# Attention and spectral mixing: the second group's weights as pairs of modes in rows of 12 KB

## The chip, the cores and the metric

The kernel runs on one core of one Trainium2 chip. The metric is device time in microseconds (us), the median of several runs; profiles come from one profiled execution, whose own time is given beside its span. Engines: PE (matmuls; PEld are its weight loads), DVE, ACT and Pool (elementwise work), SP (here it only issues DMAs). The 16 DMA engines move data between HBM and the on-chip memory of 128 partitions.

## What is computed

Sliding-window attention with a linear bias, then a mixing of its output in the frequency domain. q, k, v are [8, 8, 576, 64] (batch, head, position, depth), w_r and w_i are [64, 512, 512] (mode, in, out), w_ch is [512, 512], all float32.

```
attn[b,h] = softmax(q k^T / 8 - slope_h * |i - j|, only 0 <= i - j < 128) v
x = attn with heads side by side              # [8, 576, 512]
X = rfft(x, axis=1)                           # modes 0..63 are used
Yr = Xr w_r - Xi w_i ;  Yi = Xr w_i + Xi w_r  # per mode a 512 x 512 matrix
y = irfft(Y) ;  u = x + y
out = u + max(u w_ch, 0)
```

## The kernel before, in words

**Two groups of rows.** Heads come in four pairs, and a pair of heads is 128 of the 512 columns of x. Group 0 is the first pair, group 1 the other three (`GROUPS`, line 19). The mixing of group 0 needs only x's first 128 columns, so its weights (rows 0 to 127 of each mode's matrix) are loaded and used while the attention of group 1 still runs; the weights of group 1 (rows 128 to 511, 100.7 MB) come afterwards. All weights together are 134 MB, q, k and v 28 MB.

**Stages.** (a) `_slot` (line 537) is one step of the attention: scores (L431), exponentials on ACT (L437), masks on DVE (L445), transposes (L372, evacuated on ACT, L382), products with v (L462) and normalising on DVE (L480). Pool casts q, k and v to bf16 (`_cast`, L362). A slot also takes one step of the waiting spectra (`_spectrum1`) and at most one tile of group 0's modes (`_modes`, called with `w0` or `w1`). (b) After the last slots, the loop of lines 190 to 203 takes group 1's modes one after another, and between them fills PE with x times w_ch (`_xt`, four transposes L658, and `_xw`, L678 and L680, split by ACT and DVE into `hl`, L684 and L685), with the steps of the inverse transform's matrix (`_ft_steps`) and with the parts of the result that early modes allow (`_z_early`, L700 and L703). (c) `_finish` makes the output tiles and stores them.

**Spectra.** `_spectrum1` multiplies a batch's x by the cosine and sine matrix F on PE (L521), for group 1 in three steps a = 0, 1, 2 per batch, since the partition p of the result holds row 128 + 3p + a. After the third, DVE copies the spectrum (L528, real and imaginary) and its negated imaginary part (L529) to `Xlast` in bf16. Those of the last two batches come at the end of the attention, all in one slot.

**Modes.** `_modes` multiplies a mode's weights with the spectra: 4 blocks of outputs times A rows per partition (A = 3 in group 1) times w_r and w_i, so 24 matmuls with 128x128 weights and 16 columns (2 parts by 8 batches), added up in PSUM (`acc`). At the ends of blocks of modes the sums go to `ZTa` (float32, ACT, L645) in group 0, and with those added to `ZT` (bf16, DVE, L651) in group 1.

**The order of the work.** Every engine does its instructions in the order in which they are written (`manual_schedule`, line 95), SP's DMAs among them. The weights have a ring of three buffers for w_r and three for w_i (`RING`, 6 KB per partition each). `_load_w` (line 582) issues one DMA for w_r and one for w_i of a tile, 768 KB each: three modes of group 0 (rows of 2 KB in HBM), or one mode of group 1 (6 KB in a row: three rows of the matrix for each partition). A load waits until PE has used what was in its buffer. w_ch comes in four loads of 256 KB in four of the last slots of the attention (`_load_wch`, L602), and Pool casts them in four slots further on (`_cast_wch`, L606), before stage (b).

**The end.** Between the last four modes stand filler matmuls (`_idle`, L612, ten, ten, ten and five) whose results are not used.

Of the kernel before, what the change touches and what calls it, by code (L numbers as in the profile page):

```python
# [16 lines left out]
P = 128  # L17
# [16 lines left out]
def kernel(  # L34
# [28 lines left out]
    for grp in GROUPS:  # L63
        mg = ROWS // len(grp)
        n = NM // mg
        sizes = [mg] * n
        if NM % mg:
            sizes.insert(12, NM % mg)
        tiles.append([(sum(sizes[:i]), z) for i, z in enumerate(sizes)])
    g.ends = [{sum(t) for t in tiles[0][1::2]}, set(range(MB, NM, MB)) | {NM - 4, NM - 2}]  # L70

# [6 lines left out]
    g.FT = persist.tile([P, 4, S], BF16)  # L78
# [3 lines left out]
    g.wch = persist.tile([P, 4, DM], BF16)  # L82
    g.W, g.two, g.acc = {}, {}, {}
    g.X = [None] * len(GROUPS)
    g.X[-1] = persist.tile([P, len(GROUPS[-1]), 3, B, NM], BF16, name="Xlast")
# [9 lines left out]
    with tc.manual_schedule(engines={ET.SP, ET.PE, ET.Activation, ET.DVE, ET.Pool}):  # L95
        with ExitStack() as wctx:
            g.wpool = wctx.enter_context(tc.tile_pool(name="wpool", bufs=RING))
# [3 lines left out]
            with ExitStack() as actx:  # L101
# [3 lines left out]
                g.mask = cp.tile([P, H, 512], BF16)  # L105
                g.vns = [cp.tile([P, 2 * ST, 2, 72], BF16, name=f"vn{i}") for i in range(2)]
# [8 lines left out]
                todo = list(tiles[0])  # L115
                spare = todo.pop(0)
                loaded = (g.first[1] + LA) // 2
                for d in range(loaded):
                    _load(g, d)
                    if loaded - 2 <= d:  # L120
                        _load_w(g, 0, *todo.pop(0))
# [17 lines left out]
                with tc.tile_pool(name="spare", bufs=1, side="right") as sp:  # L139
                    _load_w(g, 0, *spare, pool=sp)  # L140
                    _load_w(g, 0, *todo.pop(0))
                    for n in range(n1, start + 1):
# [3 lines left out]
                        _slot(g, n, [], [(0, *spare)] if n == start else [])  # L146
                zx = ctx.enter_context(tc.tile_pool(name="zx", bufs=1, side="right"))
                g.ZTa = zx.tile([P, 4, 2, NM, 8], FP32)

                line = [(j, *t) for j in range(len(GROUPS)) for t in tiles[j]]  # L150
                _modes(g, 0, *tiles[0][1])
                _load_w(g, *line[RING + 1])
                ahead = RING + 2
                counts = [0, 1, 0, 1, 0, 1, 0, 1, 1, 0, 1] + [1] * (N - start - 12) + [1, 1, 1, 1]
                work, todo = {}, list(tiles[0][2:])
                for n in range(start + 1, N + 2 + TAIL):
                    work[n] = [(0, *todo.pop(0)) for _ in range(counts[n - start - 1])]
                assert not todo
                for n in range(start + 1, N + 2 + TAIL):
# [4 lines left out]
                    for _ in w:  # L164
                        _load_w(g, *line[ahead])
                        ahead += 1
                    h = (len(w) + 1) // 2
                    _slot(g, n, w[:h], w[h:])
                    if N - 7 <= n < N - 3:
                        _load_wch(g, n - N + 7)  # L170
                    if N - 2 <= n < N + 2:
                        _cast_wch(g, n - N + 2)
            zp = ctx.enter_context(tc.tile_pool(name="zpool", bufs=1, side="right"))
            g.ZT = zp.tile([P, 4, 4, 2, 16, 8], BF16)
# [4 lines left out]
            for t in line[ahead:]:  # L179
                _load_w(g, *t)  # L180
            with ExitStack() as xctx:
# [5 lines left out]
                todo, done, k = list(tiles[last]), 0, 0  # L187
                ftq = _ft_steps(g, xt, xps)
                xT = _xt(g, 0, xt, xps)
                while done < NM - 4:  # L190
                    m0, mg = todo.pop(0)
                    _modes(g, last, m0, mg, last=True)
                    done = m0 + mg
# [19 lines left out]
            for m0, mg in todo:  # L213
                _modes(g, last, m0, mg, last=True)
                if NM - 4 <= m0 < NM - 1:
                    _idle(g, BUSY)
# [61 lines left out]
def _consts2(g):  # L278
    nc = g.nc
    nc.gpsimd.tensor_tensor(  # L280
        out=g.ident2, in0=g.ident_b[:, 0:64], in1=g.ident_b[:, 64:128], op=ALU.add)
    for vn in g.vns:
        nc.gpsimd.memset(vn[:, :, :, g.D : g.D + 1], 1.0)
# [12 lines left out]
def _ft_steps(g, pool, psum):  # L296
# [7 lines left out]
    def begin():  # L304
# [4 lines left out]
        box.FTn = pool.tile([P, S], BF16, tag="FTn", name="FTn", bufs=1)  # L309
# [180 lines left out]
def _spectrum(g, d):  # L490
# [3 lines left out]
    if s == GROUPS[j][-1]:  # L494
        g.spectra += [(j, c, a) for c in (b, b + 1) for a in range(len(GROUPS[j]))]


def _spectrum1(g, j, b, a):
# [7 lines left out]
    X = g.X[j]  # L506
    nb = 4 // A
# [16 lines left out]
    if a < A - 1 or not own and b < g.B - 2 and k < nb - 1:  # L524
        return
    b0 = b - k
    if k == 0:
        nc.vector.tensor_copy(X[:, :, 1:3, b0], xt[:, 0])  # L528
        nc.vector.tensor_scalar_mul(X[:, :, 0, b0], xt[:, 0, :, 1], -1.0)  # L529
        return  # L530
    for a in range(A):
        xi = xt[:, 0 : k + 1, a].rearrange("p b i m -> p i b m")
        nc.vector.tensor_copy(X[:, a, 1:3, b0 : b + 1], xi)
        nc.vector.tensor_scalar_mul(X[:, a, 0, b0 : b + 1], xi[:, 1], -1.0)


def _slot(g, n, w0, w1):
# [16 lines left out]
    for w in w0:  # L554
        _modes(g, *w)
# [20 lines left out]
    if old:  # L576
        _av(g, d - 1, e, av)
    for w in w1:
        _modes(g, *w)


def _load_w(g, j, m0, mg, pool=None):
    nc = g.nc
    A = len(GROUPS[j])
    rows = slice(GROUPS[j][0] * P, (GROUPS[j][0] + A) * P)
    t = []
    for tag, src in (("wr", g.w_r), ("wi", g.w_i)):
        w = (pool or g.wpool).tile([P, ROWS, g.DM], FP32, tag=tag, name=f"{tag}{j}_{m0}")
        w = w[:, 0 : mg * A].rearrange("p (m a) e -> p m a e", a=A)
        nc.sync.dma_start(  # L590
            out=w.rearrange("p m a e -> p m (a e)"),
            in_=src[m0 : m0 + mg, rows].rearrange("m (p a) e -> p m (a e)", a=A))
        t.append(w)
    for i in range(mg):
        g.W[j, m0 + i] = (t[0][:, i], t[1][:, i])


def _load_wch(g, i):

    t = g.qpool.tile([P, g.R, g.D], FP32, tag="qk"[i % 2], name=f"wchf{i}")  # L600
    g.wchf = getattr(g, "wchf", []) + [t.rearrange("p r d -> p (r d)")[:, 0 : g.DM]]
    g.nc.sync.dma_start(out=g.wchf[i], in_=g.w_ch[P * i : P * i + P])  # L602


def _cast_wch(g, i):
# [234 lines left out]
```

## Time and profile before

| | before |
|---|---|
| median of 3 runs (lowest to highest) | 445.91 us (444.88 to 446.86) |
| the profiled execution: its time, its span | 446.81 us, 445.0 us |
| busy, share of the span: PE / PEld / DVE / ACT / Pool | 74% / 49% / 49% / 47% / 23% |
| read from HBM, written | 163.58 MB, 9.44 MB |
| loads of weights, 768 KB each: w_r, w_i | 85, 85 (and one of 256 KB each) |
| from issue to landing, median: w_r, w_i | 8.3 us, 9.7 us |
| PE waits for weights: w_r, w_i (L634, matmuls) | 14.0 us, 53.5 us |
| PE busy, 176 to 360 us | 112.8 of 184 us |

The profile's lines name a line of the kernel, an engine, an operation and out<-in with their shapes; "x24" counts instructions. A wait is put down to what ended it. The clock is TensorE's granted clock as a share of full speed. Slices are fortieths of the span, 11.1 us each; a digit is the busy share in tenths. A group's mean is the duration of one instruction; matmuls overlap, so that one of 0.19 us can follow another after 0.03 us.

### The profile page before, as it was taken

How to read it: one execution, taken by the hardware profiler on the slowest of the kernel's cores; microseconds unless marked ns; L12 is line 12 of the kernel's file. 1: busy time of each engine (PE TensorE's matmuls, PEld its weight loads, DVE VectorE, ACT ScalarE, POOL GpSimd, SP SyncE). 2: the span in 40 equal slices, each digit the busy share in tenths (PEclk: the TensorE clock that was granted, in tenths of full speed). 3: DMA queues.
4: the chain of work that ended last, by engine and by line, in shares of the span. 5: the costliest groups of instructions: out<-in, count | busy, mean ns of one | idle time of the engine just before them, and what ended most of it. 6: DMA issues, size and time to landing. Idle time of an engine off the chain costs nothing.

```text
span 445.0 us, 11009 instructions
## 1 busy us (share of the span) xinstructions
PE 327.6 (74%) x4626; PEld 217.1 (49%) x4654; DVE 219.2 (49%) x396; ACT 207.1 (47%) x313; POOL 101.6 (23%) x151
## 2 busy tenths in 40 slices
PE   2778889889979977467764656656665488869995
PEld 1445666666757654334443333333333355535553
DVE  6467867788758733242232323333233334512885
ACT  4799968999979501121322212212122132311884
POOL 8644535555533102000000000000000000000883
PEclk9999988999989855685566556566556669969999
DMA  8999989999999999999999999999999999992688
GB/s 294 395 389 385 404 321 399 392 404 405 406 406 402 406 409 404 417 423 425 422 423 425 419 415 418 426 423 423 424 423 423 425 410 417 416 422 122 252 313 288
DMA packets 55217, 173.73 MB, mean 390 GB/s; under 512 B 4992, under 2 KB 4992, under 8 KB 55168
## 3 DMA queue, kind: packets, MB, share of 16 engines
q1 hardware_dynamic: 55168, 173.04, 97.7%
q8 instruction: 36, 0.59, 0.5%
q14 instruction: 13, 0.11, 0.1%
HBM read 163.58 MB, written 9.44 MB: 389 GB/s over the span
## 4 chain that ended last, share of the span: by engine, by line
DMA 50%; PE 26%; ACT 12%; DVE 8%; issue 3%; SPq 1%; POOL 0%; ACTq 0%; POOLq 0%
DMA wi<-in_moe_w_i_dram 50%; PE acc L634 7%; ACT att L437 5%; ACT T L382 4%; DVE att L445 3%; PE mm L667 2%; PE idle L612 2%; PE tqk L372 2%; PE sc L431 2%; PE y L667 2%; PE xw L680 2%; PE av L462 1%; PE av L401 1%; DVE x_sb L480 1%; PE tp L658 1%
## 5 line engine op out<-in xcount | busy, mean ns | idle before, releaser
L684 ACT CAST hl<-xw 64x512 bf16<-64x512 f32 x72 | 41.8, 580 | 163.6 <-PE xw L680 126.1
L634 PEld LDWEIGHTS <-wi 128*128 128x128 bf16 x1024 | 65.7, 105 | 73.6 <-DMA wi<-in_moe_w_i_dram 71.7
L685 DVE TENSOR_TENSOR hl<-xw,hl 64x512 bf16<-64x512 f32 x72 | 49.6, 689 | 85.5 <-ACT hl L684 85.4
L634 PE MATMUL acc<-Xlast,wi 128*128 128x16 bf16 x768 | 55.9, 194 | 48.6 <-DMA wi<-in_moe_w_i_dram 48.5
L634 PEld LDWEIGHTS <-wr 128*128 128x128 bf16 x1024 | 70.7, 106 | 37.2 <-DMA wr<-in_moe_w_r_dram 26.4
L806 POOL TENSOR_TENSOR o<-r,ys 128x512 f32<-128x512 f32 x18 | 22.5, 1279 | 243.7 <-DVE r L798 242.3
L634 PE MATMUL acc<-Xlast,wr 128*128 128x16 bf16 x768 | 63.2, 194 | 19.4 <-DMA wr<-in_moe_w_r_dram 13.5
L445 DVE TENSOR_TENSOR att<-att,mask 128x1024 bf16<-128x1024 bf16 x64 | 55.9, 873 | 36.9 <-ACT att L437 36.6
L437 ACT ACTIVATE att<-sc 128x1024 bf16<-128x1024 f32 x64 | 66.7, 1043 | 9.9 <-PE sc L431 8.7
L382 ACT COPY T<-tqk 128x640 bf16<-128x640 bf16 x92 | 65.6, 767 | 1.7 <-PE tqk L372 1.7
L680 PE MATMUL xw<-wch,xT 128*128 128x512 bf16 x122 | 54.7, 577 | 4.9 <-issue 3.1
L372 PE MATMUL tqk<-ident_b,b 128*128 128x128 bf16 x432 | 39.4, 233 | 10.6 <-POOL b L362 6.4
L660 DVE COPY xT<-tp 128x512 bf16<-128x512 bf16 x36 | 15.2, 423 | 51.8 <-PE tp L658 50.8
L372 PEld LDWEIGHTS <-b 128*128 128x128 bf16 x432 | 27.3, 104 | 22.2 <-issue 11.0
L362 POOL CAST b<-v 128x576 bf16<-128x576 f32 x32 | 27.0, 871 | 17.6 <-issue 8.5
L680 PEld LDWEIGHTS <-xT 128*128 128x128 bf16 x144 | 19.0, 138 | 23.5 <-issue 21.6
L431 PE MATMUL sc<-T,T 64*128 64x256 bf16 (+2 forms) x320 | 26.9, 266 | 1.7 <-ACT att L437 1.0
L362 POOL CAST b<-q 128x576 bf16<-128x576 f32 x32 | 21.5, 699 | 28.9 <-issue 28.9
L362 POOL CAST b<-k 128x576 bf16<-128x576 f32 x32 | 22.0, 714 | 16.3 <-issue 8.5
L462 PE MATMUL av<-vn,att 128*128 128x65 bf16 (+1 forms) x576 | 25.3, 204 | 0.4 <-DVE vn L405 0.2
L462 PEld LDWEIGHTS <-att 128*128 128x128 bf16 (+1 forms) x576 | 21.3, 106 | 3.5 <-issue 0.2
L480 DVE TENSOR_TENSOR x_sb<-av,rec 128x512 bf16<-128x512 f32 x32 | 22.1, 692 | 1.1
(102 smaller groups left out, 437.8 us busy)
## 6 DMA issues: line engine op xcount, KB each, us to landing
wr<-in_moe_w_r_dram SPq DMA_DIRECT2D x85, 768.0 KB, 8.3
wi<-in_moe_w_i_dram SPq DMA_DIRECT2D x85, 768.0 KB, 9.7
q<-in_q_dram SPq DMA_DIRECT2D x32, 288.0 KB, 7.5
k<-in_k_dram SPq DMA_DIRECT2D x32, 288.0 KB, 6.1
v<-in_v_dram SPq DMA_DIRECT2D x32, 288.0 KB, 7.0
out_dram<-o SPq DMA_DIRECT2D x32, 256.0 KB, 3.0
wchf<-in_moe_w_ch_dram SPq DMA_DIRECT2D x4, 256.0 KB, 10.7
out_dram<-o SPq DMA_DIRECT2D x8, 128.0 KB, 2.7
```

The source lines that it names most:

```text
L362: g.nc.gpsimd.tensor_copy(u.b[w][:, :, e], u.raw[w][e])
L372: g.nc.tensor.transpose(u.tp[:, r - r0], u.b[w][:, r].rearrange("p u d -> p (u d)"), g.ident_b)
L382: copy(u.T[w].rearrange("c h (p r) -> c (h p) r", r=g.R)[:, :, r0:r1], u.tp[:, 0 : r1 - r0].rearrange("c r p -> c p r"))
L431: nc.tensor.matmul(sc[:, e, c0 : c0 + nq], lhsT=kT[es, h, _start(kt) : _start(kt) + P], rhs=qT[es, h, kt * P : kt * P + nq], start=True, s ...
L437: nc.scalar.activation(a, sc, AF.Exp, scale=1.0 / math.sqrt(g.D))
L445: nc.vector.tensor_tensor(out=a, in0=a, in1=m, op=ALU.mult)
L462: nc.tensor.matmul(av[o, h, t * (D + 1) : (t + 1) * (D + 1)], lhsT=u.att[min(kt // 2, 1), h][:, f, c0 : c0 + m], rhs=vn[:, g.ST * h + kt, ...
L480: nc.vector.tensor_tensor(out=xo, in0=avv[:, :, 0:4, 0:D], in1=rec[:, :, 0:4].unsqueeze(-1).broadcast_to([P, 2, 4, D]), op=ALU.mult)
L634: nc.tensor.matmul(acc[:, et, :, m - c0, :], lhsT=(wr, wi)[k][:, a].bitcast(BF16)[:, 1::2][:, et * P : (et + 1) * P], rhs=X[:, a, 1 - k : ...
L680: nc.tensor.matmul(xw, lhsT=xT[:, dt], rhs=g.wch[:, dt], start=(dt == 0 and g.way[n] != "q"), stop=(dt == 3))
L684: nc.scalar.copy(g.hl[hi, n, h], xw[hi])
L685: nc.vector.tensor_tensor(out=g.hl[lo, n, h], in0=xw[hi], in1=g.hl[hi, n, h], op=ALU.subtract)
```

## The change

Group 1's weights are loaded as items of one matrix (w_r or w_i) and two modes, m and m + 1, 1.5 MB in one DMA: partition 2q takes rows 6q to 6q + 5 of mode m, and partition 2q + 1 the same rows of mode m + 1, each 12 KB in a row in HBM. A matmul with such weights sums over both modes' rows, so the spectra are laid out with zeros: for the columns of an even mode the odd partitions hold zero, and the other way round. `_expand` makes this from the old layout (`Xc`) with a 0/1 matrix (`pick`): two matmuls, a copy on DVE and a negation on Pool for each half of the six rows, so that a batch of group 1 takes five steps of spectra, not three, and a slot may take a second one. `_pair_modes` then does a pair in 48 matmuls with 32 columns, all of w_r first, then all of w_i.

The ring is now one tile of three slots of 12 KB, the same bytes. An item is a pair's w_r or w_i, or three modes' w_r and w_i of group 0, which are still two loads with rows of 2 KB. `_send` is written behind the matmuls that free a slot. The last item is loaded in two halves.

To make room, `FT` and `wch` move to memory that is free only after the attention, `ZT` lies inside `ZTa`, and w_ch is loaded in one DMA of 1 MB behind the first pair of group 1 (`_wch`), into a part of `hl` that is filled last; Pool casts it from there. The first `_xt` moves behind that too. The filler matmuls are divided anew (ten, ten, three, five), and there are eleven output buffers instead of twelve. The core of the diff (old bodies that stand above are left out):

```diff
+    tiles.append([])
     g.ends = [{sum(t) for t in tiles[0][1::2]}, set(range(MB, NM, MB)) | {NM - 4, NM - 2}]
+    tiles[1] = [(m, w) for m in range(0, NM, 2) for w in range(2)]
...
-    g.X[-1] = persist.tile([P, len(GROUPS[-1]), 3, B, NM], BF16, name="Xlast")
+    g.X[-1] = persist.tile([P, 2 * len(GROUPS[-1]), 3, B, NM], BF16, name="Xlast")
...
-            g.wpool = wctx.enter_context(tc.tile_pool(name="wpool", bufs=RING))
+            wpool = wctx.enter_context(tc.tile_pool(name="wpool", bufs=1))
+            g.wring = wpool.tile([P, RING, 2 * ROWS * DM], FP32)
+            g.line = [(j, *t) for j in range(len(GROUPS)) for t in tiles[j]]
+            g.sent, g.used = 1, 0
...
+                g.pick = cp.tile([P, 2, 2, P], BF16)
+                g.Xc = cp.tile([P, 2, 3, 2, NM], BF16)
...
-                    for _ in w:
-                        _load_w(g, *line[ahead])
-                        ahead += 1
                     h = (len(w) + 1) // 2
                     _slot(g, n, w[:h], w[h:])
-                    if N - 7 <= n < N - 3:
-                        _load_wch(g, n - N + 7)
-                    if N - 2 <= n < N + 2:
-                        _cast_wch(g, n - N + 2)
+                    _send(g)
+            g.ZT = g.ZTa.bitcast(BF16).rearrange("p e k a m (b t) -> p e k (a m) b t", t=2)[..., 0]
+            g.FT = zp.tile([P, 4, S], BF16)
+            g.wch = zp.tile([P, 4, DM], BF16)
...
-            for t in line[ahead:]:
-                _load_w(g, *t)
...
-                todo, done, k = list(tiles[last]), 0, 0
+                todo, done, k = list(range(0, NM, 2)), 0, 0
                 ftq = _ft_steps(g, xt, xps)
-                xT = _xt(g, 0, xt, xps)
+                xT = None
                 while done < NM - 4:
-                    m0, mg = todo.pop(0)
-                    _modes(g, last, m0, mg, last=True)
-                    done = m0 + mg
+                    m0 = todo.pop(0)
+                    _pair_modes(g, m0)
+                    _send(g)
+                    done = m0 + 2
+                    if m0 == 0:
+                        _wch(g)
+                        xT = _xt(g, 0, xt, xps)
...
-            for m0, mg in todo:
-                _modes(g, last, m0, mg, last=True)
-                if NM - 4 <= m0 < NM - 1:
-                    _idle(g, BUSY)
+            for m0 in todo:
+                _pair_modes(g, m0)
+                _send(g)
...
+    nc.gpsimd.memset(g.pick, 0.0)
+    one = g.ident_b.rearrange("p (q t) -> p q t", t=2)
+    for h in range(2):
+        for t in range(2):
+            nc.gpsimd.tensor_copy(
+                g.pick[:, h, t].rearrange("p (q t) -> p q t", t=2)[:, :, t], one[:, :, h])
...
-        box.FTn = pool.tile([P, S], BF16, tag="FTn", name="FTn", bufs=1)
+        box.FTn = g.hl[:, len(g.seq) - 5].rearrange("p h d -> p (h d)")[:, 0:S]
...
-        g.spectra += [(j, c, a) for c in (b, b + 1) for a in range(len(GROUPS[j]))]
+        g.spectra += [(j, c, a) for c in (b, b + 1) for a in range(len(GROUPS[j]) + 2 * j)]
...
+    if a >= A:
+        _expand(g, X, b, a - A)
+        return
...
+    if j:
+        nc.vector.tensor_copy(g.Xc[:, b % 2], xt[:, 0])
+        return
     b0 = b - k
-    if k == 0:
-        nc.vector.tensor_copy(X[:, :, 1:3, b0], xt[:, 0])
-        nc.vector.tensor_scalar_mul(X[:, :, 0, b0], xt[:, 0, :, 1], -1.0)
-        return
-    for a in range(A):
-        xi = xt[:, 0 : k + 1, a].rearrange("p b i m -> p i b m")
-        nc.vector.tensor_copy(X[:, a, 1:3, b0 : b + 1], xi)
-        nc.vector.tensor_scalar_mul(X[:, a, 0, b0 : b + 1], xi[:, 1], -1.0)
+    xi = xt[:, 0 : k + 1, 0].rearrange("p b i m -> p i b m")
+    nc.vector.tensor_copy(X[:, 0, 1:3, b0 : b + 1], xi)
+    nc.vector.tensor_scalar_mul(X[:, 0, 0, b0 : b + 1], xi[:, 1], -1.0)
+def _expand(g, X, b, h):
+    nc = g.nc
+    A = len(GROUPS[-1])
+    if b == g.B - 1 and h:
+        xz = g.ps2.tile([P, 2, 512], FP32, tag="sc", name="xzl")[:, 0]
+    else:
+        xz = g.ps2.tile([P, 512], FP32, tag="xt", name="xz")
+    xz = xz[:, 0 : 2 * A * g.NM].rearrange("p (a i m) -> p a i m", a=A, i=2)
+    for t in range(2):
+        nc.tensor.matmul(
+            xz.rearrange("p a i m -> p (a i) m")[:, :, t::2], lhsT=g.pick[:, h, t],
+            rhs=g.Xc[:, b % 2].rearrange("p a i m -> p (a i) m")[:, :, t::2],
+            start=True, stop=True)
+    X = X[:, A * h : A * h + A]
+    nc.vector.tensor_copy(X[:, :, 1:3, b], xz)
+    nc.gpsimd.tensor_scalar_mul(X[:, :, 0, b], X[:, :, 2, b], -1.0)
...
+    if g.spectra and g.spectra[0][0]:
+        _spectrum1(g, *g.spectra.pop(0))
...
+        _modes(g, 0, *w)
+def _load_w(g, i, t):
+    sync = g.nc.sync
+    j, m, n = g.line[i]
     A = len(GROUPS[j])
     rows = slice(GROUPS[j][0] * P, (GROUPS[j][0] + A) * P)
+    if j == 0:
+        t = t.rearrange("p (w m e) -> p w m e", w=2, e=g.DM)
+        for w, src in enumerate((g.w_r, g.w_i)):
+            sync.dma_start(
+                out=t[:, w, 0:n], in_=src[m : m + n, rows].rearrange("m p e -> p m e"))
+            for x in range(n):
+                g.W[j, m + x, w] = t[:, w, x : x + 1]
+        return
+    src = (g.w_r, g.w_i)[n][m : m + 2, rows].rearrange("m (q r) e -> q m r e", r=2 * A)
+    t = t.rearrange("p (r e) -> p r e", e=g.DM)
+    h = A if i == len(g.line) - 1 else 2 * A
+    for r in range(0, 2 * A, h):
+        sync.dma_start(
+            out=t[:, r : r + h].rearrange("p r e -> p (r e)"),
+            in_=src[:, :, r : r + h].rearrange("q m r e -> q m (r e)"))
+    g.W[j, m, n] = t
+def _send(g, n=RING):
+    while n and g.sent < min(len(g.line), max(g.used, 1) + RING):
+        _load_w(g, g.sent, g.wring[:, (g.sent - 1) % RING])
+        g.sent += 1
+        n -= 1
+def _wch(g):
+    nc = g.nc
+    raw = g.hl[:, len(g.seq) - 4 :].rearrange("p n h d -> p (n h d)").bitcast(FP32)
+    raw = raw.rearrange("p (c d) -> p c d", c=4)
+    nc.sync.dma_start(out=raw, in_=g.w_ch.rearrange("(c p) d -> p c d", c=4))
+    for i in range(4):
+        nc.gpsimd.tensor_copy(g.wch[:, i], raw[:, i])
...
+            for k in range(c0 // 16, m // 16 + 1):
+                a, z = max(c0, 16 * k), min(m + 1, 16 * k + 16)
+                nc.scalar.copy(
+                    g.ZTa[:, :, k, :, a % 16 : a % 16 + z - a].rearrange("p e a m b -> p e a (m b)"),
+                    acc[:, :, :, a - c0 : z - c0].rearrange("p e a m b -> p e a (m b)"))
...
+def _pair_modes(g, m):
+    nc = g.nc
+    j = len(GROUPS) - 1
+    X = g.X[j]
+    A = 2 * len(GROUPS[j])
+    ends = g.ends[j] | {g.NM}
+    if m == 0 or m in ends:
+        g.acc[j] = (m, g.mpsum.tile([P, 4, 2, 8, 8], FP32, tag="acc", name="acc"))
+    c0, acc = g.acc[j]
+    late, end = m >= g.NM - 4, m == g.NM - 2
+    steps = [(0, et, a) for et in range(4) for a in range(A)]
+    if end:
+        steps += [(1, et, a + h) for h in (0, A // 2) for et in range(4) for a in range(A // 2)]
+    else:
+        steps += [(1, et, a) for et in range(4) for a in range(A)]
+    n = len(steps)
+    for i, (k, et, a) in enumerate(steps):
+        if late and 2 * i == n:
+            _idle(g, BUSY // 3 if end else BUSY)
+        if end and 4 * i == 3 * n:
+            _idle(g, BUSY // 2)
+        nc.tensor.matmul(
+            acc[:, et, :, m - c0 : m - c0 + 2, :],
+            lhsT=g.W[j, m, k][:, a].bitcast(BF16)[:, 1::2][:, et * P : (et + 1) * P],
+            rhs=X[:, a, 1 - k : 3 - k, :, m : m + 2].rearrange("p c b m -> p c m b"),
+            start=(i == 0), stop=(i == n - 1))
+    g.used += 2
+    if m + 2 in ends:
+        k, ms = c0 // 16, slice(c0 % 16, m % 16 + 2)
+        dst = g.ZTa[:, :, k, :, ms].rearrange("p e a m b -> p e a (m b)")
+        o = g.ZT[:, :, k].rearrange("p e (a m) b -> p e a m b", a=2)[:, :, :, ms]
+        nc.vector.tensor_tensor(
+            out=o.rearrange("p e a m b -> p e a (m b)"),
+            in0=acc[:, :, :, 0 : m + 2 - c0].rearrange("p e a m b -> p e a (m b)"),
+            in1=dst, op=ALU.add)
+    if late and not end:
+        _idle(g, BUSY)
...
-                o[j] = pool.tile([P, g.DM], FP32, tag="o", bufs=12, name="o")
+                o[j] = pool.tile([P, g.DM], FP32, tag="o", bufs=11, name="o")
```

## The prediction

> **What bounds the kernel now.** I read first the slices of the span, then a table by stage, then the chain of work that ended last.
>
> ```profile
> DMA  8999989999999999999999999999999999992688
> GB/s 294 395 389 385 404 321 399 392 404 405 406 406 402 406 409 404 417 423 425 422 423 425 419 415 418 426 423 423 424 423 423 425 410 417 416 422 122 252 313 288
> DMA 50%; PE 26%; ACT 12%; DVE 8%; issue 3%; SPq 1%; POOL 0%; ACTq 0%; POOLq 0%
> ```
>
> The DMA engines are busy through 36 slices (up to 400 us), and half of the chain is transfers. The rate has two levels: about 405 GB/s, and about 422 once only the second group's weights move. The table by stage (columns: window, length, busy us of PE, PEld, DVE, ACT, POOL, clock, DMA share, GB/s) says the same:
>
> ```profile
> 60.00:68.00 8.00, 6.79 (x107) 5.37 (x103) 3.94 (x10) 4.53 (x7) 2.67 (x3) 0.66 0.82 290
> 128.00:163.00 35.00, 31.20 (x536) 23.43 (x534) 23.72 (x48) 21.84 (x30) 7.91 (x12) 0.79 1.05 405
> 176.00:360.00 184.00, 112.76 (x1422) 70.07 (x1440) 57.87 (x103) 36.84 (x66) 0.00 (x0) 0.61 1.02 422
> 403.00:408.00 5.00, 4.87 (x64) 2.92 (x62) 0.04 (x1) 0.00 (x0) 0.00 (x0) 1.00 0.17 68
> ```
>
> So up to 403 us the time is bytes over rate, plus the holes in which the queue runs dry (one is at 60 to 68). Work on an engine costs nothing while the queue is fed, and its full length where it lets the queue drain. From 408 on PE, ACT and DVE share the end, which the change leaves nearly alone.
>
> **Rows of 12 KB.** From 128 us rows of 2 KB move at 405 GB/s, from 176 us rows of 6 KB at 422. Per engine (one of 16) that is 16 x 2048 / 405 = 80.9 ns and 16 x 6144 / 422 = 232.9 ns a row. The extra 4096 B take 152.0 ns (0.0371 ns a byte, 431 GB/s in all), which leaves 4.9 ns per row. A row of 12288 B then takes 461 ns, so 426.5 GB/s. The second group has 64 modes x 2 x 384 x 512 x 4 B = 100.7 MB: 238.5 us now, 236.0 after: **-2.5 us**. Bounds: no gain if such a row is moved in pieces (0), and 436 GB/s, the best single microsecond that I found (400 to 401 us), -7.6. The Trainium skill, DMA: Bandwidth & Descriptors, section Where 436 GB/s comes from, puts the ceiling of the 16 ports at 435 GB/s; by it at most 7.1 us could be won, and the 422 measured here stands within 3% of it.
>
> **w_ch is loaded late.** Before, its four 256 KB pieces go out from 127 to 141 us and Pool has cast the last by 152, 20 us ahead of the first use. Now one 1 MB load is put on SP's queue behind pair 0's two sends, and PE's first two x·w_ch products (L680) stand between pair 0 and pair 2. PE, in order, waits for the casts; behind it wait pair 2's matmuls, and SP's next send waits for those. What is in the queue by then are three items of 1.5 MB (3.7 us each) and w_ch (2.6 us at 405): 13.8 us, then nothing. The DMA engines idle from w_ch's last byte until the next item's first byte:
>
> ```profile
> L606 POOL CAST wch<-wchf x4: 611/616/617, 138.0 to 151.4; 128x512 bf16<-128x512 f32 x4
> 171.15 0.59 PE L658 MATMUL tp<-ident_b,x_sb 128*128 128x128 bf16 x4
> 171.54 1.91 PE L680 MATMUL xw<-wch,xT 128*128 128x512 bf16 x4
> 173.24 0.22 PE L634 MATMUL acc<-Xlast,wr 128*128 128x16 bf16 x1
> wchf<-in_moe_w_ch_dram SPq DMA_DIRECT2D x4, 256.0 KB, 10.7
> out_dram<-o SPq DMA_DIRECT2D x8, 128.0 KB, 2.7
> ```
>
> The last two lines (KB each, us from issue to landing) show that a load behind a full queue waits its turn: 256 KB took 10.7 us there, and 128 KB took 2.7 on the emptier queue of the end. The steps: landing after the last byte 0.7 (2.7 less 0.3 for the bytes and 1.7 for the start; the start is from the run's first load, issued at 0.73, whose window 0 to 4 us moved 0.67 MB, 1.7 us' worth, so bytes came from 2.3 on; I take 1.7); four casts of 0.615, 2.5; the first product's last matmul, 0.4; next transposes 0.4 (171.15 to 171.54); second product 1.7 (171.54 to 173.24, at the 0.5 clock granted there); 24 matmuls on pair 2's w_r, 0.75 (as from 170.42 to 171.15); SP 0.1; start 1.7. Sum **+8.3**. Bounds 5.5 (no start-up or landing time beyond the issue) and 10.5 (one more product's worth). The old cover, 20 us, is all gone.
>
> **Expanding the spectra.** Per batch two steps: two matmuls (192 columns), a DVE copy of 128x384 (0.55, row L528), a Pool negation; DVE's own negation (0.35, L529) goes, its first copy stays but goes to Xc. In the attention these 16 steps lie beside saturated transfers: SP waits there mostly for the DMA itself, ACT is the full engine, and loads land 8 to 11 us after issue, so a lag of some us is covered. Not covered is the last one. Now batches 6 and 7 take 163.55 to 168.09 on PE, and then group 0's last item frees its slot (SP issues at 168.99). After: spectrum 2.25, copy 0.65, expand 0.45, copy 0.6 (the PSUM tile is shared), expand 0.45, spectrum 2.3, copy 0.6, two expands 0.8, in all 8.1: 3.6 us later, issue near 172.6. The item before, issued at 163.7, has its last byte at about 173.4 (pair 0's w_i lands at 170.4 now, plus 3.7, less 0.7). The new bytes come at 172.6 + 1.7 = 174.3: a hole of 0.9, and I add 0.6 for lag from the attention: **+1.5**, bounds 0 and 5 (if PE comes 4 us late out of the attention; it waited 2.7 us for weights from 155 to 163, which is its slack).
>
> **Pool's 0/1 matrix** is one memset and four 128x64 copies ahead of the second casts: 5 x 0.3 (row L280) = 1.5 us. The hole at 60 us is set by computing, not by transfers, so half of it may arrive there: **+0.7**, bounds 0 and 1.5.
>
> **Pairs of modes.** The loads of PE weights stay 24 a mode, a matmul has 32 columns instead of 16, and both last 30 ns from one to the next when they stream (the L634 rows); at the 0.5 clock 32 columns may show, but PE is idle for a third of this stage: 0. Two z products now come in one pair. At full clock they take 1.3 us each (364.47 to 365.8) plus 0.8 for their shared tile, with a product and 48 matmuls 6.5 of the pair's 7.4 us; the first at half clock does not fit: **+0.5**, bounds 0 and 1.5.
>
> **The end.** Now the last w_i lands 9.8 us after 396.55, at 406.35, and PE is done with it at 407.93, because filler matmuls (L612) stand ahead of it. After there are 28 instead of 35, and with the last load cut in two: from the landing of mode 60's w_r (t) at half clock 0.75 + 4.5, then 0.75 + 2.2, 0.7 + 0.65, 0.36 + 1.1, so 11.0, and 0.4 behind the last landing at t + 11.15: done 0.4 after it, not 1.6: **-1.1**, bounds -1.6 and 0. Eleven output buffers instead of twelve: no store shows a wait for one, 0. Group 0's split copies on ACT (three more of some 0.4) are behind the queue's cover, 0.
>
> **Sum:** -2.5 + 8.3 + 1.5 + 0.7 + 0.5 - 1.1 = **+7.4**. The profiled execution took 446.81 (span 445.0): 454.2. The median of the three runs, 445.91, is 0.9 lower: **453.3**.
>
> **Rivals.** (1) *The queue does not run dry at w_ch*: something else reaches PE's place, or w_ch lands ahead of the items before it. Then 453.3 - 8.3 = **445.0**, no change. Against it: PE keeps its written order everywhere in the trace, and the queue its own. (2) *Faster*: large rows lift the whole stage. The other terms come to +9.9, so it decides from 100.7 MB / (238.5 - 9.9) = 440 GB/s; at 446, 225.7 us and **443.0**. For it: two sizes fix my line, and it cannot show what each load (rather than row) costs, and there are half as many. Against it: 8-us windows here never pass 428. (3) *The two modes of a load hinder each other*: neighbouring partitions read 1 MB apart. If that brings the second group back to the 405 of the first, it takes 248.5, +10.0 on now instead of -2.5: **465.8**. Group 0's loads already step 1 MB for each partition's three modes and fit 405, so I see little in it. The Trainium skill, DMA: Bandwidth & Descriptors, section Latency and other measured facts, reports large losses for copies whose rows step by large powers of two; no run here shows one. (4) *The attention lags*: expand steps, each waiting for DVE, bring PE 6.6 us late to 163 and the queue drains there: a hole of 0.9 + 6.6 = 7.5 in place of the 1.5, so **459.3**.
>
> **How the numbers follow.** Forecast 0.70 (its own range 449 to 458), rival 1 0.10, rival 2 0.07, rival 3 0.05, rival 4 0.08. The range for 8 in 10 is 447 to 460: it takes in rival 4 and the bounds of the unknown prices, and leaves out rivals 2 and 3 and part of 1. A measurement of this kernel tells about 0.5% (2.2 us) from no change: slower 0.80 (the forecast nearly whole, rivals 3 and 4), within 0.13, faster 0.07.
>
> **What would show it.** Right: in the stage from 200 us a rate of 426 or so; right after pair 0, DMA slices near zero for about 8 us, PE waiting on Pool's casts and Pool on w_ch, and a gap of some 20 us between SP's sends; the last group-0 item some 3.6 us after its old place. Wrong: a rate of 440 or 405 there, no hole, or the attention's end several us late.

## The result and the profile after

| | before | after |
|---|---|---|
| median (lowest to highest) of 4 runs each | 446.38 us (444.88 to 448.25) | 489.94 us (486.44 to 491.87) |
| ratio to before, 95% interval | 1 | 1.0965 [1.0878, 1.1052] |
| the profiled execution: its time, its span | 446.81 us, 445.0 us | 491.87 us, 490.0 us |
| end of PE's last `acc` matmul | 407.9 us | 452.8 us |

The change costs 43.6 us; the forecast was 7.4. The last row says where to look: 44.9 of the 45.0 us between the two spans are lost before the last weights are used, and the rest of the kernel takes as long as it did.

The page of the changed kernel, its slices and its chain of waits:

```profile
DMA  8999989999989989299999999999999967993488
GB/s 312 393 389 394 402 302 406 404 355 333 383 308 334 336 333 416 65 424 428 409 426 428 403 394 429 419 391 388 392 394 403 398 258 289 363 377 132 185 294 294
...
PE 41%; DMA 28%; ACT 15%; DVE 12%; issue 4%; POOL 0%; ACTq 0%; SPq 0%; POOLq 0%
```

A slice is 12.25 us here. The two even levels of before are gone. Transfers held 50% of the chain, now 28%, and PE has 41% where it had 26%. The table by stage (columns as before the change: window, length, busy us of PE, PEld, DVE, ACT, POOL, clock, DMA share, GB/s):

```profile
60.00:68.00 8.00, 6.79 (x111) 5.43 (x111) 4.22 (x10) 4.61 (x7) 2.47 (x4) 0.68 0.73 249
68.00:128.00 60.00, 51.87 (x894) 38.32 (x893) 44.49 (x80) 50.98 (x70) 31.19 (x45) 0.99 1.01 380
128.00:163.00 35.00, 29.83 (x495) 21.97 (x495) 23.49 (x45) 25.54 (x37) 11.36 (x16) 0.94 0.92 328
163.00:176.00 13.00, 11.03 (x163) 8.43 (x161) 6.96 (x15) 0.51 (x2) 2.08 (x4) 0.63 0.99 372
176.00:208.00 32.00, 16.21 (x180) 12.01 (x182) 6.27 (x12) 3.38 (x6) 6.72 (x23) 0.58 0.64 248
208.00:240.00 32.00, 21.38 (x218) 15.38 (x219) 9.00 (x19) 5.14 (x9) 0.00 (x0) 0.63 1.01 427
240.00:392.00 152.00, 108.06 (x1143) 78.78 (x1161) 45.99 (x78) 29.96 (x55) 0.00 (x0) 0.67 0.99 404
392.00:440.00 48.00, 35.89 (x522) 25.29 (x525) 16.97 (x27) 11.65 (x20) 0.00 (x0) 0.86 0.81 320
```

Before, these windows had 290, 402, 405, 402, 422, 424 and 420 GB/s, and 419 from 392 to 400; its last weights landed at 406. A missing rate times the window, over the full rate, is lost time. The attention, 60 to 176: 1.1 + 3.3 + 6.7 + 1.0 = **12.1 us**. The first pairs, 176 to 208: 174 x 32 / 422 = **13.2 us**. The long stage, against the 427 that the new rows reach from 208 to 240: 23 x 152 / 427 = 8.2, and 107 x 48 / 427 = 12.0, **20.2 us**. From this go some 2.5 us for the higher full rate. That makes 43 of the 45 us. So there are three losses, and only the second is near the size that was forecast for it (8.3).

**The first pairs.** The transfers near w_ch, in the columns of the table, and PE's and Pool's waits there (what waited, for what, us in total, times, longest):

```profile
192.00:196.00 4.00, 0.00 (x0) 0.00 (x0) 0.00 (x0) 0.00 (x0) 0.00 (x0) 0.50 1.00 402
196.00:197.60 1.60, 0.00 (x0) 0.00 (x0) 0.00 (x0) 0.00 (x0) 0.00 (x0) 0.50 0.17 65
197.60:205.80 8.20, 6.71 (x61) 4.27 (x62) 2.62 (x5) 2.32 (x4) 4.70 (x20) 0.68 0.00 1
205.80:208.00 2.20, 2.15 (x28) 1.61 (x27) 1.18 (x3) 0.58 (x1) 0.00 (x0) 1.00 0.92 246
```

```profile
POOL wch L649 <- DMA hl<-in_moe_w_ch_dram: 17.3, 1, 17.3
...
PE xw L751 <- POOL wch L649: 14.3, 1, 14.3
```

This is the forecast's hole: PE in its written order behind Pool, Pool behind w_ch, SP silent from 184.39 to 204.52. The queue is still for 8.2 us, and slow just before and after: from 196 to 208 us 10.5 us' worth of transfers at 427 GB/s is missing. The other 2.5 us lie at 176 to 184 (292 GB/s): SP's sends at the transition stand 9.3 us apart (171.00 and 180.30).

**The attention.** Slot 31's exponential begins at 160.50, before at 150.05. The lag begins at slot 17, the first with an expansion (0.65 us), is 3.4 two slots later, 8.0 at slot 25 and 10.45 at slot 31. One expansion in the timeline (start, length; the idle time before it and what ended it in brackets):

```profile
97.87 0.94 DVE L449 TENSOR_TENSOR att<-att,mask 128x1024 bf16<-128x1024 bf16 x1 [0.84 <-ACT att L441]
...
98.74 0.55 DVE L558 CAST Xlast<-xz 128x384 bf16<-128x384 f32 x1
...
99.34 0.38 PE L528 MATMUL xt<-F,x_sb 128*128 128x128 bf16 x4 [1.43 <-DVE Xlast L558]
...
100.58 1.02 ACT L441 ACTIVATE att<-sc 128x1024 bf16<-128x1024 f32 x1 [1.49 <-PE sc L435]
```

The next spectrum needs the PSUM tile of the expansion; DVE's copy out of it stands behind a mask multiplication that itself waited for ACT; PE waits 1.43 us, and the scores behind it on PE are late for ACT by 1.49. Two views of the kernel before show why little of this is made up. Its table line from 68 to 128 us, with ACT's main wait there:

```profile
68.00:128.00 60.00, 53.41 (x943) 39.55 (x940) 44.92 (x83) 54.65 (x75) 29.81 (x43) 0.98 1.04 402
...
ACT att L437 <- PE sc L431: 2.6, 4, 1.0
```

And what SP's sends waited for from 128 to 163 us, the two longest waits and the only one for a DMA:

```profile
SPq L590 <- PE acc L634: 13.2, 5, 2.8
SPq L590 <- PE av L401: 8.7, 4, 3.7
...
SPq L590 <- DMA wr<-in_moe_w_r_dram: 0.9, 2, 0.7
```

ACT was the fullest engine up to 128 us (54.7 of 60 us, PE 53.4), with little room to catch up. From 128 us on, the sends waited for PE (24.3 us in all, 0.9 for a DMA), so there a late slot means a late send.

**The long stage.** PE near the end of it:

```profile
403.78 1.56 PE L707 MATMUL acc<-Xlast,wring 128*128 128x32 bf16 x24
...
410.13 0.38 PE L771 MATMUL zwp<-wch,ZTa 128*32 128x512 bf16 x1 [1.32 <-ACT ZW L778]
410.97 0.22 PE L774 MATMUL zp<-ident_b,ZTa 128*32 128x128 bf16 x1 [0.46 <-DVE Z L777]
...
412.23 2.93 PE L707 MATMUL acc<-Xlast,wring 128*128 128x32 bf16 x48
```

Twenty-four matmuls of a pair take 1.56 us; before, 24 of a mode took 0.75. And the second of two z products in a row waits 1.3 us for ACT to empty the tile of the first. SP's sends of one matrix stand 8.8 to 9.8 us apart here (403.99, 413.81, 422.64), where the transfer of a pair takes 7.4.

### The profile page after: what moved, and what is told of

Read it like the earlier page. It is cut to its first block, busy times and chain, and to the rows that moved or that the text cites. A ratio compares the mean times of both kernels' runs of the same rounds, so it can differ in the third digit from the quotient of the medians.

```text
span 490.0 us, 10969 instructions
## 1 busy us (share of the span) xinstructions
PE 365.6 (75%) x4647; PEld 259.4 (53%) x4679; DVE 225.2 (46%) x404; ACT 207.4 (42%) x316; POOL 114.2 (23%) x172
## 4 chain that ended last, share of the span: by engine, by line
PE 41%; DMA 28%; ACT 15%; DVE 12%; issue 4%; POOL 0%; ACTq 0%; SPq 0%; POOLq 0%
DMA wring<-in_moe_w_i_dram 23%; PE acc L707 12%; ACT att L441 6%; PE xw L751 5%; DVE att L449 4%; ACT T L386 3%; DMA hl<-in_moe_w_ch_dram 3%; PE sc L435 3%; PE mm L738 2%; DVE hl L756 2%; DMA wring<-in_moe_w_r_dram 2%; PE tqk L376 2%; PE av L466 2%; PE acc L670 2%; PE y L738 2%
## 5 line engine op out<-in xcount | busy, mean ns | idle before, releaser
L707 PE MATMUL acc<-Xlast,wring 128*128 128x32 bf16 x1536 | 98.5, 236 | 48.7 <-DMA wring<-in_moe_w_i_dram 46.6
L707 PEld LDWEIGHTS <-wring 128*128 128x128 bf16 x1536 | 91.4, 120 | 66.7 <-DMA wring<-in_moe_w_i_dram 50.1
L751 PE MATMUL xw<-wch,xT 128*128 128x512 bf16 x117 | 53.5, 579 | 20.1 <-POOL wch L649 14.3
L366 POOL CAST b<-k 128x576 bf16<-128x576 f32 x32 | 23.4, 761 | 15.6 <-issue 11.3
L717 DVE TENSOR_TENSOR ZTa<-acc,ZTa 128x512 bf16<-128x512 f32 (+2 forms) x10 | 6.1, 614 | 34.5 <-PE acc L707 34.5
L559 POOL TENSOR_SCALAR Xlast<-Xlast 128x192 bf16<-128x192 bf16 x16 | 11.0, 690 | 39.1 <-DVE Xlast L558 35.0
```

The costliest lines, as they stand in the source:

```text
L366: g.nc.gpsimd.tensor_copy(u.b[w][:, :, e], u.raw[w][e])
L707: nc.tensor.matmul(acc[:, et, :, m - c0 : m - c0 + 2, :], lhsT=g.W[j, m, k][:, a].bitcast(BF16)[:, 1::2][:, et * P : (et + 1) * P], rhs=X[ ...
L751: nc.tensor.matmul(xw, lhsT=xT[:, dt], rhs=g.wch[:, dt], start=(dt == 0 and g.way[n] != "q"), stop=(dt == 3))
```

## The experiments

The theory after the result: (A) the hole at w_ch, (B) the lag of the attention, (C) matmuls whose columns lie 128 B apart, and (D) everything between two pairs now comes in one lump with no transfer free to start. The rivals for the long stage are that the large rows are slow in themselves, and that neighbouring partitions reading 1 MB apart hinder each other. The median of the changed kernel is uncertain by some 4 us (its interval), and so are differences from it; the later runs, which stand near the kernel before, are much sharper.

**e1_spread: one step of expansion per slot, the three spectrum steps together.**

```diff
         if g.spectra:
             _spectrum1(g, *g.spectra.pop(0))
+            while g.spectra and g.spectra[0][0] and g.spectra[0][2] in (1, 2):
+                _spectrum1(g, *g.spectra.pop(0))
     if old:
         _av(g, d - 1, e, av)
-    if g.spectra and g.spectra[0][0]:
-        _spectrum1(g, *g.spectra.pop(0))
```

> One expand step a slot, with the three spectrum steps of a batch together in one slot (three slots a batch instead of two and a half), so that nothing on PE comes directly behind a DVE copy that it needs. Theory: PE's waits for the shared PSUM tile make the attention late; in the changed kernel slot 31 starts 10.4 us later than before. Expected: that lag falls under 3 us, the DMA rate from 68 to 163 us is back near 400 GB/s, total 481 (489.9 less 9). Rival: the lag comes from the added work itself on DVE, Pool and PE; then it stays near 10 us and the total stays at 490.

Measured: 481.67 us, 1.0815 [1.0778, 1.0852]. Its table by stage:

```profile
68.00:128.00 60.00, 54.27 (x943) 40.50 (x943) 48.12 (x85) 53.81 (x75) 33.50 (x47) 1.00 1.05 405
128.00:163.00 35.00, 30.78 (x565) 22.90 (x563) 25.96 (x52) 22.59 (x32) 10.70 (x15) 1.00 1.01 367
```

The lag at slot 31 falls from 10.45 to 2.3 us, and the rate from 68 to 128 is that of before (402). The same work, placed so that no copy has to be waited for, loses 7 to 8 us less (by ratios and by medians): (B) is shown. What is left from 128 to 163 (367 against 405, 3.3 us' worth) is not explained by this wait.

**e2_contig: the spectra with the batch innermost, so that a matmul's columns lie side by side.**

```diff
-    g.X[-1] = persist.tile([P, 2 * len(GROUPS[-1]), 3, B, NM], BF16, name="Xlast")
+    g.X[-1] = persist.tile([P, 2 * len(GROUPS[-1]), 3, NM, B], BF16, name="Xlast")
...
-    nc.vector.tensor_copy(X[:, :, 1:3, b], xz)
+    nc.vector.tensor_copy(X[:, :, 1:3, :, b], xz)
...
-            rhs=X[:, a, 1 - k : 3 - k, :, m : m + 2].rearrange("p c b m -> p c m b"),
+            rhs=X[:, a, 1 - k : 3 - k, m : m + 2],
```

> The second group's spectra are stored with the batch innermost, so that the 32 columns of a matmul are read as two runs of 16 adjacent elements per part instead of single elements 128 bytes apart. Theory: the 61 ns between matmuls on pairs (28 to 31 ns before, with 16 columns) is the strided read of the columns. Expected: some 30 ns, 24 matmuls in 0.75 us instead of 1.55, PE less late from 208 us on, total 470 to 480. Rival: 32 columns cost 61 ns however they lie; then no change, 490.

Measured: 488.33 us, 1.0954 [1.0918, 1.0991], no gain. Three groups of its page (busy us, mean ns) and two lines of its table by stage say why:

```profile
L707 PE MATMUL acc<-Xlast,wring 128*128 128x32 bf16 x1536 | 50.5, 183 | 86.2 <-DMA wring<-in_moe_w_i_dram 69.5
...
L559 POOL TENSOR_SCALAR Xlast<-Xlast 128x192 bf16<-128x192 bf16 x16 | 26.4, 1647 | 44.0 <-DVE Xlast L558 24.7
L558 DVE CAST Xlast<-xz 128x384 bf16<-128x384 f32 x15 | 28.1, 1874 | 3.5 <-PE xz L553 3.2
```

The first two in the changed kernel, and then the lines of e2's table:

```profile
L707 PE MATMUL acc<-Xlast,wring 128*128 128x32 bf16 x1536 | 98.5, 236 | 48.7 <-DMA wring<-in_moe_w_i_dram 46.6
...
L559 POOL TENSOR_SCALAR Xlast<-Xlast 128x192 bf16<-128x192 bf16 x16 | 11.0, 690 | 39.1 <-DVE Xlast L558 35.0
```

```profile
128.00:163.00 35.00, 28.15 (x453) 20.94 (x452) 26.23 (x43) 25.09 (x36) 15.64 (x17) 0.90 0.84 295
...
240.00:392.00 152.00, 83.41 (x1184) 49.35 (x1183) 48.01 (x83) 31.63 (x57) 0.00 (x0) 0.69 1.01 423
```

PE's pair matmuls fall from 98.5 to 50.5 us in all, 24 of them from 1.55 to some 0.8, and the long stage runs at 423: (C) is real. But the same stride has only moved. DVE now writes every eighth element, 1874 ns instead of 548, Pool 1647 instead of 690, and the attention (295 from 128 to 163) gives the gain back.

**e3_late: the first x·w_ch products two pairs later.**

```diff
-                    while k < len(g.seq) and k * (NM - 4) < done * len(g.seq):
+                    while k < len(g.seq) and k * (NM - 8) < (done - 4) * len(g.seq):
```

> The first products of x with w_ch come behind the third pair of modes instead of the first; their load, casts and number are unchanged. Theory: the hole of some 10.6 us in the transfers at 196 to 207 us comes from PE's wait for the casts. Expected: no hole there, total 479 to 481 (489.9 less 9 to 10.6). Rival: the time is lost somewhere else anyway since PE has the same work in a shorter time: 486 to 490.

Measured: 479.38 us, 1.0764 [1.0724, 1.0805]; 380 GB/s from 176 to 208 (248), and no window near zero. (A) is worth 9 to 11 us, whether ratios or medians are compared.

**e4_rows6: every item of group 1 in two halves, rows of 6 KB.**

```diff
-    h = A if i == len(g.line) - 1 else 2 * A
+    h = A
```

> Every item of the second group is loaded in two halves, with rows of 6 KB instead of 12. Theory: larger rows are worth some 1% where the queue is fed (427 against 422 GB/s), so 426 to 430 falls to 422 in the windows from 208 to 240 us; total 490 to 493. Rival: the pair layout or the size of the loads itself is what makes the stage slow; then the halves, which land one by one, change the holes from 240 us on and the total by several us.

Measured: 488.32 us, 1.0961 [1.0886, 1.1035], as the changed kernel; 422 GB/s from 208 to 240 instead of 427. While something else bounds the stage, the size of the rows can't show in the time. That the large rows are slow is refuted; what they are worth had to wait for e10.

**e5_split: other work between the two halves of a pair too** (w_r's 24 matmuls, a share of the work, w_i's 24, a share), each followed by a send; the first x·w_ch products stay behind the whole first pair.

```diff
-                    m0 = todo.pop(0)
-                    _pair_modes(g, m0)
+                    m0, w0 = todo.pop(0)
+                    _pair_modes(g, m0, w0)
                     _send(g)
```

> Between the w_r half and the w_i half of a pair PE now takes part of the other work (products with w_ch, z products, transform steps), so one z product stands behind each half instead of two behind each pair. Nothing else changes. Theory: from 392 to 440 us the queue runs dry because two z products in a row, the second waiting for ACT, keep PE 9 us per pair. Expected: 370 to 400 GB/s there instead of 320, total 477 to 482. Rival: three slots of 1.5 MB are too few whatever PE does: within 3 us of 490.

Measured: 467.95 us, 1.0493 [1.0453, 1.0532], more than expected. Its table by stage:

```profile
240.00:392.00 152.00, 112.54 (x1280) 82.01 (x1297) 48.77 (x82) 32.00 (x57) 0.00 (x0) 0.71 1.00 424
```

424 GB/s with matmuls as slow as in the changed kernel (24 take 1.56 us). PE has the time, if the order is right. With one lump per pair, w_i's place comes free only behind z products, x·w_ch and 48 matmuls, and so both sends come close together and late. The order alone is worth 21 to 22 us (by ratios and by medians), about what the windows gave for the whole long stage: (D) is shown. It can't be set apart from (C) there, since e2, with the lump left as it was, also reached 423 GB/s from 240 to 392.

**e6_cbm: the spectra as they are, but the two modes of a column pair next to each other**, the sums written to PSUM in the old places.

```diff
-            acc[:, et, :, m - c0 : m - c0 + 2, :],
+            acc[:, et, :, m - c0 : m - c0 + 2, :].rearrange("p c m b -> p c b m"),
...
-            rhs=X[:, a, 1 - k : 3 - k, :, m : m + 2].rearrange("p c b m -> p c m b"),
+            rhs=X[:, a, 1 - k : 3 - k, :, m : m + 2],
```

> The 32 columns of a matmul are taken with the two modes innermost (adjacent elements of the stored spectra) and the sums are written to PSUM in that order, scattered. The stored layout stays, so the attention's copies stay at 0.55 us. Theory: what costs is the number of separate places read, now 16 runs of two elements instead of 32 single ones: 24 matmuls in 0.8 to 0.9 us instead of 1.55, and 410 to 425 GB/s from 240 to 392 us; total 476 to 482. Rival: single elements cost the same, in whatever order, or the scattered writes cost as much: 1.5 us and 488 to 490.

Measured: 478.75 us, 1.0651 [1.0533, 1.0769]. Twenty-four matmuls take 0.92 us where the granted clock is 1.0, but 1.46 at 0.5. The attention keeps its cheap copies (548 and 690 ns), so here a gain stays: 11 us by the medians, but its three runs spread from 472.69 to 479.79 us, so its size is rough.

**e7_three and e8_four: the edits together.** e7 is e1, e5 and a later start of x·w_ch (five modes, counted by halves); e8 is e7 with e6's columns.

> Three of the single edits together: expand steps one a slot, the first product with w_ch behind the third pair, and the other work between the halves. Theory: the three losses are at different places and add up: 489.9 - 8 - 10.5 - 10 = 461, so 457 to 465. Rival: they hide each other, since what one gives back the next wait takes: 468 to 475.

> The three edits and the columns with the two modes innermost. Theory: 451 to 456, still above the kernel before, since the expand steps of the last batches and Pool's matrix stay while the rows of 12 KB give only 2 to 3 us. Rival: the pairs cost nothing by themselves and the rows then win: under 446.

Measured: e7 453.78 us (449.77 to 454.44), 1.0135 [1.0063, 1.0207]; e8 449.57 us, 1.0065 [1.0045, 1.0085]. Both came out below what was expected. Three placements of unchanged work take back 36 of the 43.6 us. Alone they gave 8.3, 10.6 and 22.0, in all 40.9; that they overlap by some 5 is within the uncertainty. With the order mended the columns gain 4 us by the medians, and the spread of e7 reaches down to e8, so this gain is not shown.

**e9_end: e8, and at the end of the attention both last batches' spectra first, their four expansions behind group 0's last item, each in a tile of its own.**

```diff
+    if d > N:
+        now = [s for s in g.spectra if e or s[2] < len(GROUPS[s[0]])]
+        g.spectra = [s for s in g.spectra if s not in now]
+        for s in now:
+            _spectrum1(g, *s)
```

> The four edits together (one step of expansion per slot, first x*w_ch products later, other work between the halves of a pair, columns ordered with the two modes innermost), and the end of the attention changed: the spectra of both last batches first, their four expansions behind group 0's last item, each in a PSUM tile of its own. Theory (the end of the attention still holds up the send of the next items, because expansions stand ahead of group 0's last item): the gap between SP's sends at the transition goes back from some 10 us to about 6, and the time falls by 2.5 to 3 us against 449.6, to 446.5 to 447.5. Rival (group 0's items come late anyway, because each slot of the attention takes longer than its item): the gap only moves, and the time stays at 449 to 450.

Measured: 446.91 us (445.70 to 449.03, 10 runs; the profiled execution is the slowest of them), 1.0019 [1.0000, 1.0039], as expected: no clear difference from the kernel before. SP's sends at the transition stand 5.3 us apart, 10.0 in e8, and the time falls by 2.1 (by ratios) to 2.7 us.

**e10_rows6: e9 with e4's edit.**

> The kernel of the previous run, but every item of group 1 loaded in two halves with rows of 6 KB. Now the stage from 180 to 400 us is bound by transfers, so that the size of the rows can show. Theory (a row costs some 5 ns besides its bytes): 422 GB/s in place of 427, 2.5 to 3 us more than the previous run. Rival (the size of the rows is worth nothing, and the higher rate came from somewhere else): within 1 us of the previous run.

Measured, beside e9 on the same chip: 449.20 us, 1.0067 [1.0042, 1.0091]. The long stage of e9, then of e10:

```profile
240.00:392.00 152.00, 99.50 (x1492) 65.83 (x1489) 57.28 (x94) 36.29 (x63) 0.00 (x0) 0.84 1.01 426
```

```profile
240.00:392.00 152.00, 102.67 (x1467) 69.18 (x1465) 56.85 (x93) 36.29 (x63) 0.00 (x0) 0.83 1.02 423
```

426 against 423 GB/s, and 2.3 us by the medians: what the larger rows are worth once transfers bound the stage. The two profiled executions are equally long (449.03 and 449.12 us), so the time rests on the other runs. With the rows e10 also changes the number of loads, twice as many of half the size; the two were not tried apart.

**e12_early: e9, and two of group 0's items in slot 29, none in the last slot.**

```diff
-                counts = [0, 1, 0, 1, 0, 1, 0, 1, 1, 0, 1] + [1] * (N - start - 12) + [1, 1, 1, 1]
+                counts = [0, 1, 0, 1, 0, 1, 0, 1, 1, 0, 1] + [1] * (N - start - 12) + [1, 1, 1, 0]
+                counts[18] += 1
```

> The same kernel as the run with the changed end of the attention, but group 0's items are taken one slot earlier near the end: two of them in slot 29, none in the last slot. Theory (the remaining loss lies at the end of the attention, where group 0's last items free their places too late): 443 to 446, at or below the kernel before. Rival (the slots of the attention are the limit there, whichever slot takes an item): no difference from that run.

Measured: 448.26 us (12 runs), 1.0044 [1.0024, 1.0064]. The theory falls: taking the last items a slot earlier gains nothing. The slots themselves may be the limit from 128 to 163, where PE is busy 31.6 of 35 us in e9 and the rate stays at 360; no run tested that.

**e13_before_late: the kernel before with w_ch alone moved as in the change**, one load of 1 MB behind the loads that follow the first modes of group 1, first products behind the second mode.

> The kernel before with w_ch alone moved as in the change: one load of 1 MB behind the loads that follow the first modes of group 1, and the first x*w_ch products behind the second mode. Rows of 6 KB, modes one by one, no expansion. Theory (the late w_ch alone empties the queue): DMA near zero for 8 to 10 us shortly after the transition, 454 to 456. Rival (the hole needs the large items or the lag of the attention as well): 446 to 448.

Measured: 455.37 us, 1.0204 [1.0175, 1.0233], 9.0 us more than the kernel before. Its transfers in windows of 4 us:

```profile
180.00:184.00 4.00, 0.00 (x0) 0.00 (x0) 0.00 (x0) 0.00 (x0) 0.00 (x0) 0.50 0.90 355
184.00:188.00 4.00, 2.21 (x6) 0.57 (x6) 0.00 (x0) 0.00 (x0) 2.88 (x9) 0.50 0.04 16
188.00:192.00 4.00, 4.00 (x63) 2.76 (x61) 2.48 (x4) 1.77 (x4) 1.80 (x13) 0.64 0.06 16
192.00:196.00 4.00, 1.94 (x30) 1.24 (x28) 2.62 (x7) 1.71 (x3) 0.00 (x0) 1.00 0.87 344
```

The same hole, with rows of 6 KB, one mode at a time and no expansion. (A) needs nothing else of the change.

## Why the prediction was wrong, point by point

The sign was right, and the size was not: +7.4 forecast, +43.6 measured.

- **Rows of 12 KB (-2.5): right.** 426.5 GB/s forecast, 424 to 430 in the windows that are fed; 2.3 us by e10 against e9, for rows and number of loads together. Rival 2 (440 GB/s) and rival 3 are refuted, rival 3 by 427 GB/s from 208 to 240. What the Trainium skill reports (DMA: Bandwidth & Descriptors, section Latency and other measured facts) for rows that step by large powers of two does not show in this pattern, where neighbouring partitions read 1 MB apart but each takes 12 KB in a row.
- **w_ch late (+8.3): mechanism right, size low.** Rival 1 is refuted. It cost 10.5 us in the changed kernel, 9.0 alone in e13. Term by term: from w_ch's last byte near 197.6 to Pool's first cast at 198.21 0.6 us, where 0.7 was taken for landing; casts, two products and transposes to 202.97, 4.8 where 5.0 was taken; pair 2's 24 matmuls 1.55, not 0.75; from SP's issue at 204.52 to the first bytes near 205.8 some 1.3, not 1.7, and no 0.1 for SP. That is 8.2 us of silence, as summed, but by luck: one term too low and four slightly too high cancel. What the sum left out are the edges of the hole, some 2.2 us' worth: 65 GB/s from 196.0 to 197.6 and 246 from 205.8 to 208. (The 13.8 us of queue are 13.7 by their own terms; no term uses them.)
- **Expanding the spectra (+1.5, bounds 0 and 5): the step that failed is "a lag of some us is covered".** The windows give 11.0 us from 68 to 176 and 2.5 at the transition, e1 takes back 7 to 8 and e9 another 2 to 3. Two things failed. The lag did not stay small: slots with a step lost up to 2 us each anew, and it grew from 0.65 us to 10.45. And little of it was covered: from 68 to 163 transfers worth 10.0 us are missing for a lag of 10.45, and e1 still lacks 3.3 us' worth for a lag of 2.3. "SP waits there mostly for the DMA itself" holds from 68 to 128 us (25 of 40 us of its waits in the kernel before), but from 128 to 163, where most was lost, SP waits for PE, as the lines above show. "ACT is the full engine" holds up to 128 us too; after that it is busy 21.8 of 35 us, PE 31.2. The cost of the last steps themselves was right: the spectra and expansions of batches 6 and 7 take PE from 170.80 to 179.28, 8.5 us, where 8.1 was summed; but PE came to them 7.3 us late (163.55 before), so that SP's issue behind them came at 180.30, 11.3 us after its old place and not 3.6. Rival 4 had the lag (7.5 us, a chance of 0.08); it was priced too low and thought unlikely.
- **Pool's 0/1 matrix (+0.7): not settled.** From 60 to 68 us the rate is 249 (290 before), worth 1.1 us, but e3, with the same code up to there, has 312, and e13, without the matrix, 262.
- **Pairs of modes (+0.5, bounds 0 and 1.5): the worst step, 20 us.** Two parts of it failed, and as e2, e5 and e6 each mend most or part of the loss alone, the 20 us can't be split between them. "Both last 30 ns from one to the next" took the rows of 16 columns as good for 32: they take 1.55 us for 24, about 65 ns each, at clock 0.5 and 1.0 alike: at this stride, twice the columns, twice the time. With the columns side by side (e2) such 24 take 0.8 us. And "6.5 of the pair's 7.4 us" counted PE's work as a sum; it has to be counted from one send to the next. All work between the pairs stood in one lump in front of the matmuls that free both places, and the second z product waited for ACT besides. e5 changes the order alone and gets 21 to 22 us back.
- **The end (-1.1): right as far as it shows.** In e8, where transfers set the pace again, PE waits for the last half until 410.12 and is done 0.5 us later (0.4 forecast, 1.6 before). In the changed kernel PE was behind by then, and nothing was gained. (1.6 less 0.4 is 1.2; the sum has 1.1.)

On the columns, e2 and e6 agree in part with a rule of the Trainium skill (SBUF — State Buffer, section Door 1: The DMA port swizzle): memory is accessed in lines of 16 bytes, and full bandwidth needs two hits or more on a line. With one hit a line 24 matmuls took 1.55 us, with two 0.92 at full clock, and with the columns side by side 0.8. At half clock two hits took 1.46, which the rule doesn't tell; e6 also changes the order of the writes to PSUM, and the two were not tried apart.

## What to carry to other kernels

Larger items halve the number of points at which an engine can free a buffer and the next send can go out: put the other work between the halves of an item, and count the time from one send to the next, not the sum of the work. Before counting on a deep queue to cover a delay, look in each stage at what its sends wait for: where they wait for the engine that comes late, little is covered (a lag of 2.3 us still went with 3.3 us of missing transfers in e1). A wait that comes back in every step of a loop adds up, so look at who waits behind it, above all when that is the fullest engine. Before a layout is made for a transfer, look at the stride that each engine that reads or writes it will see: a stride taken from one engine may only move to another.

## What the hardware did that was not expected

- Matmuls of 128x32 with their columns 128 B apart: 24 in 1.55 us, at granted clock 0.5 and 1.0 alike; side by side (e2) 0.82 at 0.5 and 0.77 at 1.0; in pairs of two elements (e6) 0.92 at 1.0 and 1.46 at 0.5.
- Writing 384 bf16 a partition from PSUM on DVE took 548 ns side by side and 1874 ns at every eighth element; Pool's negation of 192 took 690 and 1647.
- The end of w_ch's load ran on about one of the 16 DMA engines: from 196.5 to 197.5 us the DMA share was 0.06 and the rate 25 GB/s.
- Nearly the same work was granted different shares of TensorE's clock from 240 to 392 us: 0.67 in the kernel before and in the changed one, 0.69 in e2, 0.71 in e5, 0.78 in e6 and e7, 0.84 in e8 and e9. Neither smaller pieces (the kernel before, e5) nor faster matmuls (e2, e6) alone go with the highest share, and no run separates why.
